# ConvNeXt-V2 block, one core: normalised rows on three of four partitions, their writes on ScalarE's queue, part of the bias add on VectorE, every third block stored whole

## The chip, the core and the metric

The kernel runs on one NeuronCore of a Trainium2 chip. The time is device microseconds (us) of one execution. The engines are PE (TensorE, matmul), ACT (ScalarE), DVE (VectorE), POOL (GpSimd) and SP (SyncE, which here only issues transfers); each takes its instructions in program order. Transfers issued by SP, ACT or POOL run on the same 16 DMA engines.

## The reference

The input is an image of 512 x 512 pixels with 96 channels, in bf16.

```python
out = depthwise 3x3 convolution of x           # 9 shifted products, per channel
h = layernorm(out) over the 96 channels        # no gain, no bias
h = gelu(h @ w1)                               # 96 -> 384
gx = sqrt(sum over all pixels of h*h + 1e-6)   # per hidden channel: needs the whole image
nx = gx / (mean of gx over channels + 1e-6)
h = gamma * (h * nx) + beta + h
return x + h @ w2                              # 384 -> 96
```

The sum over all pixels splits the work in two: nothing of the last product can start before every pixel's `h` has been made once.

## The kernel before

A block is four image rows (2048 pixels); there are 128 blocks. The kernel has two stretches.

**First stretch.** Slots `s` (loop at L826) each do several things for different blocks, one slot apart: load x of block s+4; transpose it on DVE (`turn_x`); convolve block s on PE and evacuate it with ACT (`y_bf`); square it on POOL (`ysq`) and sum over channels on PE; for each batch of four blocks make 1/sqrt(variance) in a dozen small POOL steps (`stage_rstd`, `stage_newton`), write it to DRAM and read it back spread over partitions (`stage_rows`, `stage_bcast`, tile `rbc`); multiply on POOL (`stage_norm`, tile `yn`); write `yn` to DRAM in four transfers, one for each image row (`stage_write`); one slot later read it back with the 96 channels on partitions 0 to 95 (`stage_read`, tile `ynT`); two slots after the read multiply it with w1 on PE and apply gelu on ACT (tile `g`). In a steady slot ACT does one `y_bf` and eight gelu activations: two-bank ones for units 0, 4 and 8, one-bank ones for units 2, 3, 6, 7, 10 and 11, with `y_bf` between units 7 and 8. Sums of squares come from DVE (`bst`, bn_stats) for the first two to four quarters of a block and from PE (`gram`) for the rest; `cm_quads` says how many.

What is kept for the second stretch differs by block. A whole block (`is_whole`: number modulo 10 is 0, 3 or 7, and below 114; 35 blocks) has its `g` written to DRAM in three parts (`store_next`, tile `g_dram`, one part a slot). Five blocks are held in SBUF. For the other 88 only `yn` is in DRAM, and `g` is made again.

All SP transfers stand in one queue in this order in a slot: load x, read `ynT`, write `yn` (four), `rbc`, rows, store. A transfer waits, in its queue, for what it depends on, and everything behind it waits too.

**Second stretch** (loop at L1008, `ORDER` mixes the kinds of blocks evenly). For each block: `load_rest` fetches `gl` (a whole block, POOL's queue) or `ynT` (SP's queue; 128 rows of 2048 values, that is the 96 of this block and the first 32 of the next, whose rows of w1 are zero); `load_xr` fetches x again (POOL's queue); POOL adds the bias to x (`stage_xb`, tile `xb`, f32); PE multiplies `ynT` with w1 again and ACT applies gelu (tile `gr`, four activations of 128x1536 a block); PE multiplies with the scaled w2 in four sub-blocks of 12 matmuls each, into one of two PSUM banks by turns; DVE adds `xb` and writes `o_sb`; SP writes `o_sb` out. There are four `o_sb`, five `xr` and three `xb` buffers.

In the built program each SP or ACT transfer also waits for an earlier one that used the same of eight semaphores; that is mostly the transfer eight before it in the common order of both queues.

Of the kernel before, what the change touches and what calls it, by code (L numbers as in the profile page):

```python
# [8 lines left out]
ALU = mybir.AluOpType  # L9
# [9 lines left out]
NHELD = 5  # L19
WHOLE = (0, 3, 7)  # L20
NTAIL = 14
# [35 lines left out]
def kernel(  # L57
# [39 lines left out]
    def is_whole(q):  # L97
        return q < TAIL0 and q % 10 in WHOLE

    def cm_quads(q):  # L100
        if is_whole(q) or is_held(q):
            return NQ
        if q > HELD[0]:
            return 1
        return 2 if q >= NBLK - 16 or (q - 1) % 10 in WHOLE else 3

# [15 lines left out]
    def yn_src(q):  # L122
        return yn_dram[q].rearrange("c (r w) -> c r w", r=GR)

    def yn_rows(q):
        return yn_dram[q:q + 2].rearrange("q c (r w) -> (q c) r w", r=GR)[0:128]

# [10 lines left out]
    rowsel = consts.tile([128, GR], bf16, name="rowsel")  # L138
    w1_raw = consts.tile([C, E], bf16, name="w1_raw")
    w1p = consts.tile([128, E], bf16, name="w1p")  # L140
# [43 lines left out]
    with ExitStack() as p1:  # L184
# [68 lines left out]

        cen = consts.tile([C, 128], bf16, name="cen")
        xtpool = pc.enter_context(tc.tile_pool(name="xt", side="right", bufs=1))
# [27 lines left out]
        def load_rest(n, sq, pq):  # L283
            q = ORDER[n]
            v = grp.setdefault(q, {})
            if is_held(q):
                v["g"] = gs[q]
            elif is_whole(q):
                v["g"] = late.gl.tile([128, NQ, NCH, QW], bf16, name="gl")
                pq.dma_start(out=v["g"][:].rearrange("p t j w -> p (t j w)"), in_=g_dram[whole.index(q)])  # L290
            else:
                ynt = yn_ring[SLOTS[nth_made[q] % NYT]]
                if q not in KEPT:
                    sq.dma_start(out=ynt[:], in_=yn_rows(q))
                v["ynt"] = ynt
# [24 lines left out]
        def stage_xb(q, pq, bias):  # L320
            if q is None:
                return
            xb = late.xb.tile([128, PXP, C], f32, name="xb")
            pq.tensor_tensor(out=xb[:], in0=grp[q]["xr"][:],  # L324
                                    in1=bias[:, None, :].to_broadcast([128, PXP, C]), op=ALU.add)
            grp[q]["xb"] = xb

        def stage_mm2(n, q):
# [3 lines left out]
            for sub in range(NSUB):  # L332
                O = out_bank()
                for gl_ in range(GPS):
                    gg = sub * GPS + gl_
                    for j in range(NCH):
                        t, c = gg // GQ, gg % GQ * 128
                        pe.matmul(O[:, gl_, :], lhsT=g[:, t, j, c:c + 128], rhs=W2s[:, j, :],
                                   start=(j == 0), stop=(j == NCH - 1))
                dve.tensor_tensor(out=o_sb[:, sub * GPS:(sub + 1) * GPS, :], in0=O,  # L340
                                   in1=xb[:, sub * GPS:(sub + 1) * GPS, :], op=ALU.add)
                if n == NBLK - 1:
# [44 lines left out]
        pool.memset(cen[:], 1.0)  # L387
        pool.memset(w1p[C:128, :], 0.0)
        dve.memset(SG, 0.0)
# [24 lines left out]
        for i in range(NI):  # L414
            act.dma_start(out=w1_raw[i:C:NI, :], in_=w1[chans(i), :])
        act.dma_start(out=w2_sb[:], in_=w2.rearrange("(j p) c -> p j c", p=128))
# [4 lines left out]
        def setup_ynt():  # L421
            for t in yn_ring:
                pool.memset(t[C:128, :, :].rearrange("p r w -> p (r w)").bitcast(f32), 0.0)

        def setup_mlp():
# [6 lines left out]
            dve.scalar_tensor_tensor(out=w1p[:C, :], in0=w1m[:C], scalar=-1.0 / C, in1=w1_raw[:],  # L432
                                     op0=ALU.mult, op1=ALU.add)
# [392 lines left out]
        for s in range(last_slot + 1):  # L826
            get = lambda kind: at.get((s, kind), [])
            if s + 4 < NBLK:
                load_x(s + 4)
            for b in get("read"):  # L830
                stage_read(b)
            for b in get("write"):
                stage_write(b)
            for k in get("bcast"):
                stage_bcast(k)
            for k in get("rows"):
                stage_rows(k)
            store_next()
            for k in get("newton"):
                stage_newton(k, pool)  # L840
# [4 lines left out]
            for k in get("rstd"):  # L845
                stage_rstd(k, pool)
            mlp = get("mlp")

# [36 lines left out]
            else:  # L885
# [4 lines left out]
                conv(0)  # L890
                unit(0, 2)
                unit(2, 1)
                squares(0)
# [158 lines left out]
```

## Time and profile before

| | |
|---|---|
| three timed runs | 1486.81, 1480.27, 1486.15 us; median 1486.15 |
| profiled execution, first to last instruction | 1480.8 us (the page gives no other time of it) |
| ACT busy | 1414.4 us (96%) |
| PE busy | 1391.3 us (94%) |
| POOL busy | 1300.3 us (88%) |
| DVE busy | 1182.0 us (80%) |
| granted PE clock | 0.994 |
| DMA | 433.08 MB, mean 292 GB/s |
| first stretch, steady part | about 120 to 880 us |
| second stretch | from 975 us, where the first `o_sb` is written |

The page's shares are over both stretches, which have different limits; the table by windows shows them apart. "Busy" of PE counts pipelined matmuls whose ends are modelled. A wait is put down to the semaphore that came last. Nearly all instructions carry L35, the line of the helper that records them, so they are told apart by tile.

### The profile page before, as it was taken

Reading aid. Unit: us, or ns where it says so; the run is one execution under the profiler, and the core shown is the slowest. Engines: PE = TensorE matmul, PEld = TensorE weight load, DVE = VectorE, ACT = ScalarE, POOL = GpSimd, SP = SyncE. Lnnn points to the kernel's source line nnn. Section 1 sums busy time; section 2 is a strip of 40 time slices with the busy share of each in tenths; the row PEclk is TensorE's granted clock in tenths of the full one; section 3 lists DMA queues with packets and bytes.
Section 4 is the critical chain, followed back from the end, with each engine's and each line's share of the span. In section 5 each row is a group of like instructions: output and inputs, shape, how many; then the busy total and the mean of one; then the engine's idle time right before and its main releaser. Section 6 shows DMA issues by size and latency. Waiting matters only on the chain.

```text
span 1480.8 us, 54225 instructions
## 1 busy us (share of the span) xinstructions
PE 1391.3 (94%) x23125; PEld 810.4 (55%) x23125; DVE 1182.0 (80%) x2135; ACT 1414.4 (96%) x1595; POOL 1300.3 (88%) x922
## 2 busy tenths in 40 slices
PE   8888999999999999999999997789999999999998
PEld 3434444444444444444444445467777777776776
DVE  7849989999999999999999987965555555555555
ACT  7888989999999999999999999999999999999997
POOL 3459889998998999998999987569999999999997
PEclk9999999999999999999999999999999999999999
DMA  5568788788888888888888866669999999999997
GB/s 180 179 205 255 241 253 280 228 271 260 260 248 264 258 264 255 276 253 254 263 258 266 263 216 195 195 225 409 366 359 402 417 416 413 419 410 417 411 412 282
DMA packets 167768, 433.08 MB, mean 292 GB/s; under 512 B 31558, under 2 KB 81318, under 8 KB 163046
## 3 DMA queue, kind: packets, MB, share of 16 engines
q1 hardware_dynamic: 151284, 326.04, 66.3%
q0 software_dynamic: 14880, 103.43, 17.6%
q8 instruction: 181, 2.97, 0.8%
q14 instruction: 61, 0.50, 0.1%
q10 hardware_dynamic: 1362, 0.15, 0.1%
HBM read 273.30 MB, written 156.22 MB: 290 GB/s over the span
## 4 chain that ended last, share of the span: by engine, by line
PE 30%; ACT 24%; DMA 19%; POOL 13%; DVE 6%; issue 4%; SPq 4%; POOLq 0%; ACTq 0%; DVEq 0%
PE PS L35 30%; ACT g L35 16%; DMA out_dram<-o_sb 9%; POOL yn L35 6%; ACT y_bf L35 5%; POOL ysq L35 5%; SPq L35 4%; DMA yn_dram<-yn 3%; DVE bst L35 3%; DMA xin<-in_x_dram 2%; DMA rbc<-r_dram 2%; DMA ynT<-yn_dram 1%; DMA g_dram<-g 1%; DVE o_sb L35 1%; ACT xT L35 1%
## 5 line engine op out<-in xcount | busy, mean ns | idle before, releaser
L35 ACT ACTIVATE g<-PS 128x512 bf16<-128x512 f32 (+2 forms) x1062 | 727.7, 864 | 16.5 <-PE PS L35 15.6
L35 DVE BATCH_NORM_STATS2 bst<-g 128x6 f32<-128x512 bf16 x1110 | 671.3, 672 | 35.4 <-ACT g L35 34.5
L35 PE MATMUL PS<-ynT,w1p 128*128 128x512 bf16 x2181 | 609.6, 381 | 23.6 <-ACT g L35 5.4
L35 ACT ACTIVATE gr<-PS 128x1536 bf16<-128x1536 f32 x360 | 498.5, 1459 | 18.8 <-PE PS L35 13.8
L35 POOL TENSOR_TENSOR yn<-y_bf,rbc 128x1536 bf16<-128x1536 bf16 x126 | 391.3, 3108 | 77.3 <-ACT rbc L35 21.9
L35 DVE TENSOR_TENSOR o_sb<-PS,xb 128x384 bf16<-128x384 f32 x512 | 277.3, 556 | 227.0 <-PE PS L35 190.1
L324 POOL TENSOR_TENSOR xb<-xr,B2c 128x1536 f32<-128x1536 bf16 x118 | 368.1, 3133 | 4.3 <-DVE o_sb L35 2.0
L35 PE MATMUL PS<-xT,Wq 64*32 64x511 bf16 (+1 forms) x9198 | 340.5, 389 | 26.2 <-ACT y_bf L35 8.1
L35 POOL TENSOR_TENSOR ysq<-y_bf 128x1536 bf16<-128x1536 bf16 x114 | 313.6, 2752 | 12.8 <-ACT y_bf L35 12.8
L35 PEld LDWEIGHTS <-w1p 128*128 128x128 bf16 x2181 | 171.6, 98 | 222.0 <-issue 133.4
L35 PEld LDWEIGHTS <-gr 128*128 128x128 bf16 x4296 | 212.1, 98 | 68.9 <-issue 12.0
L35 PE MATMUL PS<-W2s,gr 128*128 128x96 bf16 x4224 | 223.5, 206 | 8.2 <-DVE o_sb L35 8.0
L35 PEld LDWEIGHTS <-Wq 64*32 64x32 bf16 x9216 | 111.9, 90 | 193.3 <-issue 145.9
L35 ACT ACTIVATE y_bf<-PS 128x1536 bf16<-128x1536 f32 (+2 forms) x135 | 199.4, 1482 | 17.4 <-PE PS L35 13.3
L35 DVE STREAM_TRANSPOSE xT<-xin 128x576 f32<-128x576 f32 (+1 forms) x256 | 181.4, 748 | 8.1 <-DMA xin<-in_x_dram 8.1
L35 PEld LDWEIGHTS <-g 128*128 128x128 bf16 x1704 | 104.9, 98 | 86.3 <-issue 54.3
L35 PE MATMUL PS<-w1p,ynT 128*128 128x256 bf16 (+2 forms) x822 | 125.8, 273 | 8.0 <-ACT xT L35 3.2
L35 PE MATMUL PS<-g 128*128 128x128 bf16 x1464 | 122.6, 220 | 2.9 <-DVE PS L35 2.6
L35 PEld LDWEIGHTS <-gl 128*128 128x128 bf16 x1680 | 82.8, 98 | 26.8 <-issue 5.0
L35 PE MATMUL PS<-W2s,gl 128*128 128x96 bf16 x1680 | 89.5, 206 | 3.4 <-DVE o_sb L35 3.2
L35 PEld LDWEIGHTS <-ynT 128*128 128x128 bf16 x822 | 64.1, 97 | 31.5 <-issue 13.7
L279 POOL DMA_DIRECT2D xr<-in_x_dram x115 | 63.7, 555 | 14.2 <-POOL xb L324 14.2
(105 smaller groups left out, 576.5 us busy)
## 6 DMA issues: line engine op xcount, KB each, us to landing
xin<-in_x_dram SPq DMA_DIRECT2D x126, 432.0 KB
g_dram<-g SPq DMA_DIRECT2D x105, 512.0 KB
gl<-g_dram POOLq DMA_DIRECT2D x35, 1536.0 KB, 11.3
yn_dram<-yn SPq DMA_DIRECT2D x512, 96.0 KB
ynT<-yn_dram SPq DMA_DIRECT2D x128, 384.0 KB
out_dram<-o_sb SPq DMA_DIRECT2D x127, 384.0 KB
xr<-in_x_dram POOLq DMA_DIRECT2D x123, 384.0 KB, 6.9
ynT<-yn_dram SPq DMA_DIRECT2D x85, 512.0 KB
```

The source lines that it names most:

```text
L35: r = f(*a, **k)
L279: pq.dma_start(out=xr[:], in_=x[0, r0:r0 + GR].rearrange("r w c -> (r w) c").rearrange("(p g) c -> p g c", g=PXP))
L324: pq.tensor_tensor(out=xb[:], in0=grp[q]["xr"][:], in1=bias[:, None, :].to_broadcast([128, PXP, C]), op=ALU.add)
```

## The change

Four things are changed.

1. `ynT` holds channel 3c+i on partition 4c+i, so three of every four partitions are in use over the whole range 0 to 127; w1 is laid out the same way, and the fourth partitions are zero. A read of a block (`read_yn`) is now three transfers of 32 rows, in both stretches, and in the second stretch no rows of the next block are read.
2. In slots of the first stretch that have gelu units of a block below 114, the four `yn` writes are issued by ACT, between its activations: after unit 0, after unit 4, after `y_bf`, after unit 8. SP's order becomes load x, `rbc`, rows, store, read. Other slots keep SP, with reads first.
3. In the second stretch POOL adds the bias to three of four sub-blocks only (12 of 16 pixels of a partition). For the fourth DVE adds the bias into PSUM and then x, two instructions for one. `xr` has six buffers in place of five, since it is read until the block's end.
4. Whole blocks are those whose number is divisible by 3: 38 in place of 35, so 85 blocks are made again and not 88. `cm_quads` follows.

```diff
-WHOLE = (0, 3, 7)
+WHOLE = 3
     def is_whole(q):
-        return q < TAIL0 and q % 10 in WHOLE
+        return q < TAIL0 and q % WHOLE == 0
...
-        return 2 if q >= NBLK - 16 or (q - 1) % 10 in WHOLE else 3
+        return 2 if q >= NBLK - 16 or (q - 1) % WHOLE == 0 else 3
...
     def yn_src(q):
-        return yn_dram[q].rearrange("c (r w) -> c r w", r=GR)
-
-    def yn_rows(q):
-        return yn_dram[q:q + 2].rearrange("q c (r w) -> (q c) r w", r=GR)[0:128]
+        return yn_dram[q].rearrange("(c i) (r w) -> i c r w", i=NI, r=GR)
+
+    def read_yn(eng, t, q):
+        for i in range(NI):
+            eng.dma_start(out=t[i:128:4], in_=yn_src(q)[i])
...
                 if q not in KEPT:
-                    sq.dma_start(out=ynt[:], in_=yn_rows(q))
+                    read_yn(sq, ynt, q)
...
-            xb = late.xb.tile([128, PXP, C], f32, name="xb")
-            pq.tensor_tensor(out=xb[:], in0=grp[q]["xr"][:],
-                                    in1=bias[:, None, :].to_broadcast([128, PXP, C]), op=ALU.add)
+            n = PXP - GPS
+            xb = late.xb.tile([128, n, C], f32, name="xb")
+            pq.tensor_tensor(out=xb[:], in0=grp[q]["xr"][:, :n, :],
+                                    in1=bias[:, None, :].to_broadcast([128, n, C]), op=ALU.add)
...
+                add = xb
+                if sub == NSUB - 1:
+                    dve.tensor_tensor(out=O, in0=O, in1=B2c[:, None, :].to_broadcast([128, GPS, C]), op=ALU.add)
+                    add = grp[q]["xr"]
                 dve.tensor_tensor(out=o_sb[:, sub * GPS:(sub + 1) * GPS, :], in0=O,
-                                   in1=xb[:, sub * GPS:(sub + 1) * GPS, :], op=ALU.add)
+                                   in1=add[:, sub * GPS:(sub + 1) * GPS, :], op=ALU.add)
...
-        pool.memset(w1p[C:128, :], 0.0)
+        pool.memset(w1_raw[:], 0.0)
...
-            act.dma_start(out=w1_raw[i:C:NI, :], in_=w1[chans(i), :])
+            act.dma_start(out=w1_raw[i:128:4, :], in_=w1[chans(i), :])
...
-        def stage_write(b):
+        def write_parts(b, eng):
             yn = yns.pop(b)
-            for r in range(GR):
-                sp.dma_start(out=yn_dst(b, r), in_=yn[32 * r:32 * r + 32, :, :])
+            return [lambda r=r: eng.dma_start(out=yn_dst(b, r), in_=yn[32 * r:32 * r + 32, :, :]) for r in range(GR)]
...
-            sp.dma_start(out=t[:C], in_=yn_src(b))
+            read_yn(sp, t, b)
...
-            for b in get("read"):
-                stage_read(b)
-            for b in get("write"):
-                stage_write(b)
+            mlp = get("mlp")
+            steady = bool(mlp) and mlp[0] < TAIL0
+            wparts = [f for b in get("write") for f in write_parts(b, act if steady else sp)]
+            if not steady:
+                for b in get("read"):
+                    stage_read(b)
+                while wparts:
+                    wparts.pop(0)()
             for k in get("bcast"):
                 stage_bcast(k)
             for k in get("rows"):
                 stage_rows(k)
             store_next()
+            if steady:
+                for b in get("read"):
+                    stage_read(b)
...
                 unit(0, 2)
+                write_next()
                 unit(2, 1)
...
                 unit(4, 2)
+                write_next()
                 squares(1)
...
                     evac()
+                write_next()
                 gram_next(1 if taps else 2)
                 unit(8, 2)
+                write_next(len(wparts))
                 unit(10, 1)
...
-                late.xr = p2.enter_context(tc.tile_pool(name="xr", side="right", bufs=5))
+                late.xr = p2.enter_context(tc.tile_pool(name="xr", side="right", bufs=6))
```

More of the change, by code (lines that the diff above doesn't have):

```diff
@@ L138 @@
     rowsel = consts.tile([128, GR], bf16, name="rowsel")
-    w1_raw = consts.tile([C, E], bf16, name="w1_raw")
+    w1_raw = consts.tile([128, E], bf16, name="w1_raw")
     w1p = consts.tile([128, E], bf16, name="w1p")
@@ L252 @@
             dve.tensor_copy(out=eye32[32 * q:32 * q + 32, :], in_=ident_f[32 * q:32 * q + 32, 32 * q:32 * q + 32])
-        cen = consts.tile([C, 128], bf16, name="cen")
+        cen = consts.tile([128, 128], bf16, name="cen")
         xtpool = pc.enter_context(tc.tile_pool(name="xt", side="right", bufs=1))
@@ L422, in setup_ynt @@
             for t in yn_ring:
-                pool.memset(t[C:128, :, :].rearrange("p r w -> p (r w)").bitcast(f32), 0.0)
+                pool.memset(t[:].rearrange("p r w -> p (r w)").bitcast(f32), 0.0)
         def setup_mlp():
@@ L431, in setup_mlp @@
                           start=(j == 0), stop=(j == NCH - 1))
-            dve.scalar_tensor_tensor(out=w1p[:C, :], in0=w1m[:C], scalar=-1.0 / C, in1=w1_raw[:],
+            dve.scalar_tensor_tensor(out=w1p[:], in0=w1m, scalar=-1.0 / C, in1=w1_raw[:],
                                      op0=ALU.mult, op1=ALU.add)
@@ L838, with write_next @@
             store_next()
+            if steady:
+                for b in get("read"):
+                    stage_read(b)
+            def write_next(n=1):
+                for f in wparts[:n]:
+                    f()
+                del wparts[:n]
             for k in get("newton"):
@@ L846 @@
                 stage_rstd(k, pool)
-            mlp = get("mlp")
             def spread_out():
```

## The prediction

> **What bounds the kernel now.** I read the page first for the two stretches, then the busy time by windows for the engine that is full in each, then the waits, then SP's own waits, and last the timeline at the places that the change touches. Busy time by windows (PE, PEld, DVE, ACT, POOL, clock, DMA share, GB/s):
>
> ```profile
> core 0: us, PE busy (x) PEld busy (x) DVE busy (x) ACT busy (x) POOL busy (x), PEclk, DMA share, GB/s
> 320.00:480.00 160.00, 154.30 (x2805) 76.20 (x2790) 159.25 (x275) 160.00 (x228) 147.85 (x106) 1.00 0.83 258
> 480.00:640.00 160.00, 153.19 (x2772) 74.70 (x2772) 159.00 (x274) 159.05 (x227) 152.00 (x118) 1.00 0.83 260
> ```
> ```profile
> 1000.00:1440.00 440.00, 429.06 (x6255) 317.52 (x6252) 240.80 (x445) 423.19 (x307) 423.37 (x255) 1.00 1.01 405
> ```
>
> In the first stretch ACT is never idle (160.00 of 160), DVE hardly, and DMA has room (0.83). In the second, PE, ACT and POOL are each at 96 to 98%, the DMA engines are full, and only DVE has room (55%). Who waits there, from the list of waits (total, times, longest):
>
> ```profile
> DVE o_sb L35 <- DMA out_dram<-o_sb: 35.4, 24, 2.7
> ...
> ACT g L35 <- PE PS L35: 15.6, 15, 3.4
> ...
> PE PS L35 <- DVE o_sb L35: 11.3, 15, 1.6
> ```
>
> DVE waits for an output buffer whose write has not landed, PE then waits for DVE's bank: late transfers reach PE. The prices, from the page's groups and issues:
>
> ```profile
> L35 ACT ACTIVATE gr<-PS 128x1536 bf16<-128x1536 f32 x360 | 498.5, 1459 | 18.8 <-PE PS L35 13.8
> ...
> L35 DVE TENSOR_TENSOR o_sb<-PS,xb 128x384 bf16<-128x384 f32 x512 | 277.3, 556 | 227.0 <-PE PS L35 190.1
> L324 POOL TENSOR_TENSOR xb<-xr,B2c 128x1536 f32<-128x1536 bf16 x118 | 368.1, 3133 | 4.3 <-DVE o_sb L35 2.0
> ```
> ```profile
> gl<-g_dram POOLq DMA_DIRECT2D x35, 1536.0 KB, 11.3
> ...
> ynT<-yn_dram SPq DMA_DIRECT2D x85, 512.0 KB
> ```
>
> **The second stretch.** DMA: 85 reads of 512 KB (44.6 MB) become 82 reads of 384 KB (32.2 MB); three more whole blocks add 4.7 MB. That is 7.6 MB less; at the window's 405 GB/s, 18.8 us. ACT: three blocks fewer are made again, 12 activations at 498.5/360 = 1.385 us, 16.6 us less. PE: 36 matmuls of 512 columns fewer; three in a row span 0.81 us in the timeline and one record is 0.38, so they are 0.215 apart: 7.7 us less. PE idles 440 - 429.06 = 10.9 us in the window, so if every idle stretch went too PE could give 18.6 us, the same as DMA. POOL: 125 adds of 3.13 us lose a quarter, 98 us; POOL stops being one of the full engines, so its own 16.6 us of idle and its pace no longer matter.
>
> DVE: one more add of 0.557 us a block, 71 us over 128 blocks. In the window (440 us, 112 blocks at 3.9 us) that is 62 us, from 55% to 69%: room enough, but not free of effect. The bank of the last sub-block is held for two adds, 1.11 us, where it was held for 0.56. PE wants that bank again after one sub-block of 12 matmuls (24 in a row span 1.18 us, so 0.51) and, in two blocks of three, one group of three remaking matmuls (0.65): 1.16 us. So the second add is just covered, and where it is not PE loses up to 0.1 us, with 0.6 where no group lies between. Bounds 0 and 128 x 0.1 = 13 us; I take 3, since the average fits. The three reads for one cost SP two more issues of 0.33 us a block, in a queue that mostly waits for `o_sb`; reads are issued five blocks (20 us) ahead, which hides them unless SP is held by an earlier transfer. `xr` is released a block later and has a sixth buffer for it: 0.
>
> Bounds of the stretch: the limits of DMA and PE (18.8) less nothing, and PE's 7.7 alone less 13, that is 5 us worse. I take 15 us gained: the common limit less 3 for the bank, and a little of the late writes left.
>
> [...]
>
> **The first stretch.** What moves is 440 `yn` writes out of SP's queue into ACT's, the full engine. Four prices.
>
> (a) The issue. A write's issue takes 0.598 us (median of 379 between 160 and 840 us, longest 2.7): 263 us of ACT's queue in all. Whether ACT computes meanwhile is seen at the start, where ACT issues loads behind activations:
>
> ```profile
> 5.42 0.44 ACT L35 ACTIVATE Wq<-g 32x288 bf16<-32x288 bf16 x1 [1.46 <-DVE g L35]
> 5.59 0.59 ACTq L35 DMA_DIRECT2D w_raw<-in_w_dram  x1
> 5.77 0.88 ACT L35 ACTIVATE Wq<-g 32x288 bf16<-32x288 bf16 x2
> ```
>
> In program order the loads follow all six activations, yet the first issue runs while the first of them does: the queue issues while the engine works off what it has in hand. Each new write stands behind an activation of 1.1 us (two banks) or 1.56 us (`y_bf`), longer than 0.6. Bounds 0 and 263; I take 0, by this row, the same engine and the same operation. If that cover is gone, each write costs 0.6 us.
>
> (b) The wait for `yn`. The first write of a slot waits for POOL, and behind it stand unit 2 and all later activations. POOL after a batch's small steps, and ACT in the same slot:
>
> ```profile
> 516.40 3.11 POOL L35 TENSOR_TENSOR yn<-y_bf,rbc 128x1536 bf16<-128x1536 bf16 x1
> ```
> ```profile
> 515.52 5.94 ACT L35 ACTIVATE g<-PS 128x1024 bf16<-128x1024 f32 x9
> ```
>
> `yn` is ready at 519.51. The nine activations are units 8, 10, 11 and then 0, 2, 3, 4, 6, 7 of the next slot; unit 0 starts at 517.5 and unit 2 at 518.4. With the write between them unit 2 would start at 519.51 + 0.6: 1.7 us lost. That is one slot in four, 27 batches: upper bound 46 us. But a lost 1.7 us stays gained for POOL, whose work for four slots takes 27.6 us (from one batch's small steps at 511.88 to the next at 539.49) where ACT's takes 28.2 (`y_bf` at 507.12, 514.19, 521.25). One delay serves all later batches. I take 3.
>
> (c) The wait for an earlier transfer on the same semaphore. A slot had about 8.5 transfers and will have 10.5, so the one eight before is about 7.05 x 8/10.5 = 5.4 us old. The chain of waits shows pieces of 5.89 us for an x load and 7.03 for a `ynT` read, so some writes will come up to 1.6 us too early, and ACT has 0.5 to 1.6 us in hand. Bounds 0 and one such wait of 1.1 us in each of 110 slots, 121; I take 4, since a 128 KB read and a write that no longer stands behind three others should land sooner than those pieces.
>
> (d) What SP gets back:
>
> ```profile
> SPq L35 <- DMA yn_dram<-yn: 133.5, 149, 3.8
> ...
> SPq L35 <- POOL yn L35: 64.3, 39, 4.2
> ```
>
> SP stands 64 us for POOL's `yn`, with `rbc`, rows and stores behind it, and POOL waits for `rbc` 21.8 us in turn. With the writes gone `rbc` goes out at once and POOL runs earlier, which helps (b). For the end only ACT's idle time counts: 680 - 671.04 = 9.0 us between 160 and 840 us. Bounds 0 and 9; I take 4.
>
> [...]
>
> Edits taken at nothing: 4.7 MB more stores (DMA share 0.83 covers them), three bn_stats fewer, memsets over 128 partitions (POOL is done with them by 12.2 us and next waits for ACT until 34.2), the w1 load behind a memset that ends before 2.8 us.
>
> Net of the first stretch: +3 + 4 - 4 = 3 us worse.
>
> **Sum.** -15 + 3 = -12 us. Against the profiled execution, 1480.8 - 12 = 1468.8. Its span lies 5.35 us under the median of the runs shown, near the fastest of them, so for the median I say 1486.15 - 12 = 1474 us.
>
> **Rivals.** A difference of 0.5% is 7.4 us, about what three runs of this kernel can tell from none.
>
> Slower: ACT's queue becomes the bound of the first stretch. One mechanism, (c): reads wait for the last write, the write of the next slot waits for a read, the x load stands behind both. For it: ACT has no idle time, two more transfers a slot, landings of 6 to 7 us. Against: 5.4 us and what ACT has in hand cover most. At 0.3 us a slot it is 33 us: 1486 - 15 + 33 = 1504. It decides from 22.4 us on, 0.2 us a slot.
>
> Faster by more: (b) and (c) cost nothing, ACT's 9 us of idle go, and the second stretch gains the whole 18.8: 1486 - 28 = 1458. For it: POOL and SP are relieved in both stretches.
>
> No change: the second stretch gives PE's 7.7 alone, since ACT and PE at 97% hold each other, and the first costs 8 by (b) and (c): 1486.
>
> **How the numbers follow.** Forecast 0.44 (own range 1466 to 1478), faster by more 0.15, no change 0.17, slower 0.24. So faster 0.59, same 0.17, slower 0.24. The range 1456 to 1500 reaches the middle of the faster case and most of the slower one; about 0.2 stays outside.
>
> **What would show it.** Right: between 1000 us and the end DMA share still near 1 but `o_sb` waiting less than 35 us for output, POOL near 78%, 348 `gr` activations; in the first stretch `y_bf` still every 7.05 us and ACT idle under 10 us. Wrong: `y_bf` further apart than 7.25 us with ACT's idle time ended by a transfer or by POOL's `yn` (the slower case); more than 13 us of PE waiting for `o_sb` (the bank). The prediction fails most easily if the earlier-transfer wait recurs in every slot.

## The result and the profile after

The changed kernel takes 1626.22 us (median, 1621.01 to 1630.46) against 1483.32 us (1480.26 to 1486.81) for the kernel before, measured beside it: a ratio of 1.0955, 95% interval 1.0927 to 1.0982. It is slower by 143 us, where 12 us less was forecast, and far outside the range of 1456 to 1500. The profiled execution has a span of 1628.4 us (before: 1480.8).

Both stretches lost. I count the second stretch from the first `o_sb` add to the last: it begins at 1099.4 us (before 975.5, so the first stretch is 123.9 us longer) and lasts 525.7 us (before 501.9, 23.8 longer).

The busy time by windows of the changed kernel: two windows of the first stretch, two of the second.

```profile
core 0: us, PE busy (x) PEld busy (x) DVE busy (x) ACT busy (x) POOL busy (x), PEclk, DMA share, GB/s
320.00:480.00 160.00, 139.66 (x2434) 67.76 (x2432) 140.56 (x239) 141.93 (x198) 131.92 (x100) 0.97 0.79 235
480.00:640.00 160.00, 139.61 (x2381) 66.51 (x2388) 137.43 (x232) 140.03 (x195) 126.56 (x99) 0.94 0.78 231
...
1240.00:1360.00 120.00, 117.19 (x1688) 85.51 (x1687) 82.71 (x152) 112.85 (x81) 93.46 (x71) 1.00 1.01 396
1360.00:1440.00 80.00, 76.60 (x1111) 56.07 (x1108) 53.33 (x99) 73.47 (x54) 54.31 (x42) 1.00 1.00 373
```

In the first stretch no engine is full any more: ACT, which had 160.00 of 160, has 141.93, and the DMA share fell with it. Every engine has room and the work is slower, so the time is in waits between them. `y_bf` comes every 8.21 us on the mean between 320 and 800 us, against 7.10, and ACT idles 58.7 of these 480 us, against 3.9. In the second stretch the DMA share is still 1.0, yet the rate is 373 to 396 GB/s where it was 414 in both windows. The kernel before, in its second stretch:

```profile
1120.00:1240.00 120.00, 116.87 (x1703) 86.46 (x1702) 64.89 (x121) 115.11 (x84) 116.71 (x70) 1.00 1.02 413
1240.00:1360.00 120.00, 116.66 (x1690) 85.83 (x1689) 65.42 (x122) 114.71 (x84) 116.09 (x72) 1.00 1.02 414
1360.00:1440.00 80.00, 77.08 (x1126) 57.12 (x1125) 43.38 (x81) 76.13 (x56) 76.63 (x47) 1.00 1.02 414
```

The waits of the changed kernel over the whole run (total, times, longest):

```profile
POOL yn L35 <- DMA yn_dram<-yn: 76.6, 32, 4.5
POOL xb L326 <- DMA xr<-in_x_dram: 51.8, 15, 4.9
...
ACT g L35 <- PE PS L35: 44.4, 67, 2.1
ACT g L35 <- DMA ynT<-yn_dram: 39.2, 29, 2.8
...
DVE o_sb L35 <- POOL xb L326: 26.8, 24, 2.9
...
PE PS L35 <- DVE o_sb L35: 18.9, 16, 2.2
```

and SP's own:

```profile
SPq L35 <- DMA yn_dram<-yn: 356.4, 132, 7.7
```

ACT, whose activations need no transfer, waits for `ynT` reads: these are its writes, standing in its queue. DVE's wait for output buffers is nearly gone (35.4 to 2.8 us), and another has come: POOL for `xr`, and DVE for POOL's `xb`. SP's wait for POOL's `yn` is gone (64.3 to 2.5), its wait for the landing of `yn` writes is up from 133.5 to 356.4. One slot in the timeline, ACT and then SP:

```profile
606.59 0.56 ACTq L35 DMA_DIRECT2D yn_dram<-yn  x1
607.19 1.09 ACT L35 ACTIVATE g<-PS 128x512 bf16<-128x512 f32 x2
608.16 1.46 ACT L35 ACTIVATE y_bf<-PS 128x1536 bf16<-128x1536 f32 x1
611.57 0.56 ACTq L35 DMA_DIRECT2D yn_dram<-yn  x1
612.17 1.02 ACT L35 ACTIVATE g<-PS 128x1024 bf16<-128x1024 f32 x1 [2.56 <-DMA ynT<-yn_dram]
```
```profile
602.59 0.38 SPq L35 DMA_DIRECT2D g_dram<-g  x1
609.21 1.73 SPq L35 DMA_DIRECT2D ynT<-yn_dram  x3
```

SP stood from 602.97 to 609.21 for the last write of the block that it was to read; ACT had issued that write at 602.56, and it landed at 609.06. SP's reads went out at 609.21, the first of them landed at 611.54, and ACT's next write, which shares a semaphore with it, could be issued only at 611.57. ACT had been free since 609.62.

### The profile page after: what moved, and what is told of

Read it like the earlier page. It is cut to its first block, busy times and chain, and to the rows that moved or that the text cites. A ratio compares the mean times of both kernels' runs of the same rounds, so it can differ in the third digit from the quotient of the medians.

```text
span 1628.4 us, 55038 instructions
## 1 busy us (share of the span) xinstructions
PE 1431.7 (88%) x23104; PEld 822.3 (50%) x23104; DVE 1265.6 (78%) x2260; ACT 1423.6 (87%) x1583; POOL 1205.0 (74%) x925
## 4 chain that ended last, share of the span: by engine, by line
PE 24%; DMA 19%; DVE 6%; ACT 5%; POOL 2%; SPq 2%; issue 2%; ACTq 1%; POOLq 0%; DVEq 0%
PE PS L35 24%; DMA xr<-in_x_dram 6%; ACT g L35 4%; DMA ynT<-yn_dram 4%; DMA yn_dram<-yn 4%; DVE o_sb L35 3%; DVE PS L35 2%; SPq L35 2%; DMA xin<-in_x_dram 2%; DMA out_dram<-o_sb 1%; DMA g_dram<-g 1%; ACTq L35 1%; POOL xb L326 1%; ACT y_bf L35 1%; POOL yn L35 1%
## 5 line engine op out<-in xcount | busy, mean ns | idle before, releaser
L35 DVE BATCH_NORM_STATS2 bst<-g 128x6 f32<-128x512 bf16 x1107 | 679.0, 673 | 148.1 <-ACT g L35 147.2
L35 PE MATMUL PS<-ynT,w1p 128*128 128x512 bf16 x2142 | 621.2, 390 | 113.9 <-ACT g L35 83.4
L35 ACT ACTIVATE gr<-PS 128x1536 bf16<-128x1536 f32 x348 | 488.6, 1449 | 51.0 <-PE PS L35 45.9
L35 PE MATMUL PS<-xT,Wq 64*32 64x511 bf16 (+1 forms) x9198 | 348.8, 397 | 30.9 <-ACT y_bf L35 16.0
L326 POOL TENSOR_TENSOR xb<-xr,B2c 128x1152 f32<-128x1152 bf16 x118 | 280.5, 2392 | 86.7 <-DMA xr<-in_x_dram 51.8
L35 DVE TENSOR_TENSOR o_sb<-PS,xb 128x384 bf16<-128x384 f32 x384 | 209.1, 556 | 124.4 <-PE PS L35 83.9
L35 ACT ACTIVATE y_bf<-PS 128x1536 bf16<-128x1536 f32 (+2 forms) x135 | 191.3, 1422 | 17.7 <-PE PS L35 13.4
L35 PE MATMUL PS<-W2s,gl 128*128 128x96 bf16 x1824 | 100.6, 208 | 23.4 <-DVE o_sb L35 18.4
L35 PEld LDWEIGHTS <-gl 128*128 128x128 bf16 x1824 | 91.5, 99 | 52.9 <-issue 29.5
L35 DVE TENSOR_TENSOR PS<-PS,B2c 128x384 f32<-128x384 f32 x128 | 72.5, 566 | 50.9 <-PE PS L35 50.9
```

The source lines that it names most:

```text
L35: r = f(*a, **k)
L326: pq.tensor_tensor(out=xb[:], in0=grp[q]["xr"][:, :n, :], in1=bias[:, None, :].to_broadcast([128, n, C]), op=ALU.add)
```

## The experiments

Times are set against runs of the kernel before on the same chip. The table has the stretches (us), each from one profiled execution. How far these can be trusted: eight kernels of this document, the one before among them, have the same second stretch, and it lasted 501.2 to 505.2 us. For late_xr and three_plain the profiled execution was the fastest of its kernel, 10 and 7 us below the median.

| kernel | second stretch begins | lasts | ratio of times (95%) |
|---|---|---|---|
| before | 975.5 | 501.9 | 1 |
| changed | 1099.4 | 525.7 | 1.0955 (1.0927 to 1.0982) |
| writes_only | 1041.8 | 502.0 | 1.0418 (1.0368 to 1.0468) |
| layout_only | 1043.8 | 497.3 | 1.0411 (1.0367 to 1.0454) |
| adds_only | 979.1 | 523.4 | 1.0177 (1.0135 to 1.0219) |
| whole_only | 975.0 | 507.6 | 1.0018 (0.9988 to 1.0047) |
| after_writes_sp | 1046.3 | 522.3 | 1.0564 (1.0520 to 1.0607) |
| after_one_layout | 1039.4 | 530.7 | 1.0622 (1.0568 to 1.0676) |
| three_plain | 1020.5 | 501.5 | 1.0345 (1.0289 to 1.0401) |
| writes_read_later | 1104.7 | 502.7 | 1.0881 (1.0837 to 1.0925) |
| writes_early | 1202.4 | 505.2 | 1.1551 (1.1501 to 1.1601) |
| second_add | 976.1 | 511.8 | 1.0063 (1.0035 to 1.0091) |
| late_xr | 974.5 | 509.5 | 1.0094 (1.0065 to 1.0122) |
| reads_96 | 972.0 | 525.6 | 1.0135 (1.0100 to 1.0169) |
| layout_second | 985.4 | 497.2 | 0.9994 (0.9972 to 1.0017) |
| layout_second_b | 975.8 | 497.1 | 0.9974 (0.9950 to 0.9998) |

### The four parts, one at a time

**Only the writes on ScalarE's queue** (writes_only: the kernel before, plus this; an excerpt):

```diff
+            wparts = [f for b in get("write") for f in write_parts(b, act if steady else sp)]
...
                 unit(0, 2)
+                write_next()
...
```


> The kernel before with one part of the change: in the steady slots the four yn writes of a block are issued from ScalarE's queue at the new places, and the read of a slot goes out behind the broadcast, the rows and the stores. The ynT reads stay single transfers of 96 rows, so a slot has about 8.5 transfers and not 10.5. In the changed kernel the second stretch began at 1099.4 us and before at 975.5: 123.9 us were lost in about 110 steady slots, 1.1 us a slot. Theory 1 (ScalarE waits at a write for an earlier transfer, read or write, whatever the number of reads): this part alone costs at least 60 us, y_bf periods of 7.6 us or more, total 1545 or more. Theory 2 (the two added reads are what fills SP's queue and the semaphores; the move of the writes alone is harmless): within 15 us of before, y_bf periods of 7.1 us. Theory 3 (the two need each other): 10 to 50 us. The second stretch should stay at 502 us under all three.

1547.49 us: the first stretch loses 66.3 us, the second nothing. Theory 1 holds in size: this part is enough alone. (It also puts the read behind `rbc`, rows and store in SP's order, as the changed kernel does; that was not tried by itself.) Its waits:

```profile
ACT g L35 <- DMA ynT<-yn_dram: 26.0, 13, 3.2
...
ACT g L35 <- DMA yn_dram<-yn: 8.7, 3, 3.6
```
```profile
SPq L35 <- DMA yn_dram<-yn: 454.6, 163, 9.5
```

I followed every write through the semaphore that it shares. Between 320 and 800 us 15 of 246 writes left ACT idle for more than 0.1 us before they were issued (I call these held up), 17.0 us together, and each was issued 0.02 to 0.08 us after the landing of the transfer that had used its semaphore before: ten were `ynT` reads, issued by SP after 4 to 7 us of standing, within 0.15 us of the landing of a `yn` write that ACT had issued 5 to 7 us earlier. None came with POOL's `yn`. The issue behind a late write is not covered: 9.0 us for the 15, that is 0.60 each. The other 231 left ACT idle for 7.4 us, 0.03 each.

**Only the layout** (layout_only: three reads for one, in both stretches; writes on SP; an excerpt):

```diff
+    def read_yn(eng, t, q):
+        for i in range(NI):
+            eng.dma_start(out=t[i:128:4], in_=yn_src(q)[i])
...
-            sp.dma_start(out=t[:C], in_=yn_src(b))
+            read_yn(sp, t, b)
```


> The kernel before with one part of the change: yn on three of four partitions, so that each ynT is read by three transfers of 32 rows, from SP's queue as before; the writes stay on SP. A slot of the first stretch then has about 10.5 transfers. Theory 1 (the loss is in ScalarE's queue): first stretch as before, second stretch begins at 975 to 985 us. Theory 2 (the reads fill SP's queue and the semaphores): SP, which stood 133 us for its own yn writes, stands much longer and the first stretch loses 60 us or more. Theory 3 (the two need each other): 0 to 30 us lost. For the second stretch, which took 525.7 us in the changed kernel against 501.9: if the three spread reads slow the transfers down (262 us of them more in packets of gl, 547 ns against 482), it is longer by 15 to 30 us here already; if the other parts do it, it gains some 10 us from 11 MB less read.

(The "262 us" in it is a slip; nothing rests on it.) 1546.98 us: 68.3 us lost in the first stretch, 4.6 gained in the second. Theory 2 is right here in the loss, without any write on ACT, but not in its sign: SP did not stand longer for its `yn` writes. SP issues transfers for 406.9 of the 480 us between 320 and 800 us, against 336.4: 6.4 us a slot of 7.56 and not 5.0 of 7.10. A read's issue takes 0.60 us on the mean, three times, where the single one took 0.45. SP's wait for `yn` writes fell from 133.5 to 67.4 us. The end of that chain in the waits (all of the run), first of layout_only, then of the kernel before:

```profile
ACT g L35 <- PE PS L35: 63.6, 50, 5.3
...
POOL yn L35 <- DMA rbc<-r_dram: 49.8, 15, 10.4
...
PE PS L35 <- POOL ysq L35: 45.5, 25, 5.8
```
```profile
POOL yn L35 <- DMA rbc<-r_dram: 21.8, 9, 7.2
...
PE PS L35 <- POOL ysq L35: 10.2, 5, 4.0
```

`rbc` comes late, POOL's `yn` and the `ysq` behind it are late, PE waits for POOL, and ACT waits for PE (15.6 us before).

**Only VectorE's adds and the sixth `xr` buffer** (adds_only; the excerpt leaves out POOL's shorter add and the buffer).

```diff
+                if sub == NSUB - 1:
+                    dve.tensor_tensor(out=O, in0=O, in1=B2c[:, None, :].to_broadcast([128, GPS, C]), op=ALU.add)
+                    add = grp[q]["xr"]
```


> The kernel before with one part of the change: for the last sub-block of each block VectorE adds the bias and then x itself, GpSimd prepares three quarters of xb, and xr has a sixth buffer. The first stretch is not touched: second stretch from 975 us. If the later release of xr and the bank held for two adds are what makes the second stretch longer in the changed kernel, it grows here by 10 to 25 us, with GpSimd waiting for xr (51.8 us in the changed kernel). If they are hidden, as the forecast took, the time is within 5 us of before, GpSimd near 78% busy.

1510.81 us, and the loss is in the second stretch: +21.5 us. This part is what the second stretch of the changed kernel lost, though POOL has 87.68 of 120 us busy where it had 116.71.

**Only every third block stored whole** (whole_only; an excerpt).

```diff
-WHOLE = (0, 3, 7)
+WHOLE = 3
```


> The kernel before with one part of the change: every third block is stored whole, 38 in place of 35. 4.7 MB more are written in the first stretch and read in the second, three 512 KB reads fewer, 12 activations of 1.385 us and 36 matmuls of 512 columns fewer in the second stretch. By the forecast's rows: DMA +4.7 - 1.6 = 3.1 MB, 8 us more at 405 GB/s, against 8 to 17 us less of TensorE and ScalarE: between 8 us slower and 8 us faster, by whether the DMA or the engines bound. The even spacing in place of 0, 3, 7 of ten should change nothing.

1486.16 us, no change that can be told: the interval of the ratio allows 2 us less to 7 us more. The profiled execution has 5.7 us more in the second stretch, although 12 activations and 36 wide matmuls are fewer.

By stretch the four nearly add up: in the first 66.3 + 68.3 + 3.6 - 0.5 = 137.7 (together 123.9), in the second 0.1 - 4.6 + 21.5 + 5.7 = 22.7 (together 23.8).

### Two parts undone

The changed kernel with the writes back on SP (after_writes_sp), and the changed kernel with the old layout and single reads (after_one_layout), both as excerpts.

```diff
-            wparts = [f for b in get("write") for f in write_parts(b, act if steady else sp)]
...
+            for b in get("write"):
+                stage_write(b)
```


> The changed kernel with one part undone: the writes are back on SP's queue, in the order of before. One part alone cost 66.3 us (writes) and 68.3 us (layout) in the first stretch, and both together 123.9; in the second stretch writes 0, layout -4.6, VectorE's adds +21.5, every third block whole +5.7, and all four together +23.8. Theory 1 (the parts add up): the second stretch begins at 1040 to 1050 us (68 late), lasts 520 to 528 us, total 1562 to 1580. Theory 2 (one cause, SP's full queue, of which each part is a different view): it begins well below that, under 1025 us, or takes back less than 40 us of the changed kernel's loss, over 1060.

```diff
-                    read_yn(sq, ynt, q)
+                    sq.dma_start(out=ynt[:], in_=yn_rows(q))
```


> The changed kernel with the other part undone: yn on the 96 partitions of before, one transfer for each read, while the writes stay on ScalarE's queue. If the parts add up, the second stretch begins at 1035 to 1050 us, as with the writes moved alone, and lasts some 529 us (+21.5 and +5.7 without the layout's -4.6): total 1568 to 1585. If it is the three issues of a read that make ScalarE's waits what they are, the second stretch begins below 1025 us.

1570.47 and 1575.54 us. Undoing the writes gives back 53.1 us of the first stretch, undoing the layout 60.0: two losses, not two views of one. But the layout's loss has another form beside the writes: SP then issues for 219.3 of 480 us only and is not full. Between 320 and 800 us POOL waits 55.3 us for buffers that a `yn` write still holds (18.9 with the old layout) and ACT's held-up writes are 27 with 22.5 us (23 with 18.2). That this comes of the thirds' later landing is likely, not shown.

### Number of reads or layout

Three_plain is the kernel before with each read of the first stretch split in three, on the old partitions.

```diff
+            for i in range(NI):
+                sp.dma_start(out=t[32 * i:32 * i + 32], in_=yn_src(b)[32 * i:32 * i + 32])
```


> The kernel before with each ynT read of the first stretch cut in three transfers of 32 rows; the rows stay on partitions 0 to 95, so the layout is that of before, and the reads of the second stretch are left single. The kernel with only the new layout lost 68 us in the first stretch; SP's issues took 407 of 480 us there between 320 and 800 us (6.5 us a slot) against 336 (4.9 us a slot). Theory 1 (the number of issues fills SP's queue): the same 55 to 70 us are lost here, the second stretch begins at 1030 to 1046 us. Theory 2 (the spread partitions themselves make the transfers slow): it begins at 975 to 990 us.

1535.06 us; the second stretch begins 45.0 us late, between the two. The number of issues makes about two thirds of the layout's 68.3 us. The rest goes with the spread rows, whose issues are longer: 0.60 us against 0.45 for a third of plain rows, so that a slot's reads add 1.36 us of issuing to SP's queue in layout_only and 0.89 in three_plain. The two losses stand in the same ratio as these two numbers, which speaks for the time of issuing, without proving it.

### Why ScalarE's writes wait

Both kernels are writes_only with one more change: the reads one slot later (writes_read_later), or the writes earlier (writes_early).

```diff
-                put(s + 2, "read", b)
+                put(s + (2 if ramp else 3), "read", b)
```


> The kernel with only the writes moved to ScalarE's queue, and on top of that each ynT read is put one slot later (it still has a slot before the block's matmuls). In the kernel with only the writes moved, SP stood 454.6 us for yn writes that ScalarE had just issued, and ScalarE stood 26 us for ynT reads at its own writes; its second stretch began at 1041.8 us, 66 us late. Theory 1 (a closed loop: ScalarE's last write of a slot lands, only then SP issues the read, and the next slot's write stands for that read on the shared semaphore): the read finds its write landed, the loop opens, SP's wait for yn falls below 150 us and at least 45 of the 66 us come back; second stretch from 975 to 995 us. Rival A (ScalarE pays for the issue, 0.60 us for each of four writes a slot, or for GpSimd's yn, whatever the reads do): the second stretch still begins at 1030 us or later. Rival B (eight semaphores are shared whatever the order): between the two, 1000 to 1030.

```diff
                 unit(0, 2)
-                write_next()
+                write_next(2)
...
```


> As with only the writes moved to ScalarE's queue (second stretch from 1041.8 us), but two of the four writes stand at the first place and two at the second, none later. Between 320 and 800 us 15 of that kernel's writes were held up, each until 0.02 to 0.08 us after the landing of the transfer that used its semaphore before, ten of them a ynT read that SP had issued late, because it stood 4 to 7 us for the last, fresh write. Theory 1 (fresh writes hold SP, SP's late read holds the next write): with the last write some 4 us earlier SP finds it landed, its wait for yn falls from 455 us to 250 or less, and 30 to 60 of the 66 us come back: second stretch from 980 to 1010 us. Rival A (issuing four times 0.6 us on ScalarE's queue is itself the cost): two writes in a row are less covered than one, and it begins at 1040 us or later. Rival B (some other transfer takes the read's place on the semaphore, as when the reads were put later): 1020 us or later, with ScalarE waiting for an x load, rows or a store.

My theory 1 fell here. Each should have spared SP the standing behind a fresh write; 1614.91 and 1714.33 us were measured, worse than with the writes moved alone, although SP's wait for `yn` writes went from 454.6 to 194.4 us with later reads (with earlier writes only to 399.6). The waits, first of the later reads, then of the earlier writes:

```profile
ACT g L35 <- DMA xin<-in_x_dram: 58.9, 25, 4.1
```
```profile
SPq L35 <- DMA yn_dram<-yn: 194.4, 57, 9.5
SPq L35 <- DVE rt L35: 161.3, 24, 10.3
```
```profile
ACT g L35 <- DMA yn_dram<-yn: 87.1, 17, 6.5
...
ACT g L35 <- DMA rbc<-r_dram: 39.2, 9, 6.0
```

With later reads another transfer took the read's place: the held-up writes (31, 31.4 us between 320 and 800 us) wait for rows (5.2 us), before which SP had stood 7 to 12 us, and for the x loads behind them (25.8). With earlier writes there are 28, and 52.2 us when the idle time of two writes in a row is counted once; the list of waits puts most of it down to the `yn` writes themselves, but followed through the semaphores 25.6 us are still for `ynT` reads and 20.5 for `rbc`. Rival A has a part in it: ACT was idle for another 37.3 us of these 480 while it issued (14.7 in writes_only), where the second of two writes has no activation to cover it. Again each of these was issued within 0.08 us of the landing of the transfer before it on the same semaphore. So what holds ACT is not one loop through the read: a write in ACT's queue stands for whatever transfer is about eight before it, and that one stands in SP's queue behind anything SP waits for.

**Fewer transfers: one write for four.** This was to lift the transfer eight before out of reach. First at the first place (writes_one), then at the last (writes_one_late), then on SP with the new layout (layout_writes_one), then on SP with the old (sp_writes_one). (The first expectation speaks of 24 held-up writes in writes_only; the trace shows 15.)

```diff
-            return [lambda r=r: eng.dma_start(out=yn_dst(b, r), in_=yn[32 * r:32 * r + 32, :, :]) for r in range(GR)]
+            return [lambda: eng.dma_start(out=yn_dram[b].rearrange("(c i) (r w) -> r c i w", i=NI, r=GR), in_=yn[:])]
```


> As the kernel with only the writes moved to ScalarE's queue (second stretch from 1041.8 us, 66 us late, 24 of its 246 writes between 320 and 800 us held up), but the block's yn goes out as one transfer in place of four, at the first of the four places. A slot then has about 5.5 transfers, and the one eight before is over a slot old. Theory 1 (a write on ScalarE's queue stands for the transfer eight before it, which may itself stand in SP's queue behind something late): ScalarE's waits for transfers go below 10 us in all and the second stretch begins at 975 to 990 us. Rival A (ScalarE pays for the issue itself: 384 pieces then take four times 0.6 us in one): 1030 us or later. Rival C (the write waits for GpSimd's yn, and all the waiting now falls on this first place): 990 to 1025, with ScalarE's idle time ended by yn.

> The same single write at the last of the four places, behind the activation of banks 8 and 9, so that SP's read at the start of the next slot comes as soon after the write as with the writes moved alone. It tells the two halves of theory 1 apart. If the number of transfers is what matters (eight semaphores), the second stretch begins at 975 to 995 us although SP stands for the fresh write; if it is SP's standing behind a fresh write that makes everything late, 1010 us or later, and SP's wait for yn stays above 300 us.

> As the kernel with only the new layout (three reads for one; second stretch from 1043.8 us, 68 us late, SP issuing for 407 of 480 us), but the block's yn goes out from SP's queue as one transfer in place of four. If SP's queue was full because of the number of issues, about 2 us of issuing a slot go, SP issues for some 290 of 480 us and the second stretch begins at 975 to 985 us; the second stretch stays at 497 us, so the total is some 1473 to 1482, below the kernel before by up to 8. If one issue of four times the pieces takes four times as long, or the three reads for other reasons hold the first stretch, it begins at 1020 us or later.

> The kernel before with the block's yn written by one transfer in place of four, on SP's queue as before: the control of the run above. SP was not full before (336 of 480 us), so the forecast is no change, 975 us to the second stretch and a total within 8 us of before; a gain of up to 9 us (ScalarE's idle time in the first stretch) if GpSimd's wait for the broadcast rows, which stand behind the writes, was worth anything.

1700.35, 1798.04, 1940.77 and 1783.06 us (ratios 1.150, 1.216, 1.312 and 1.205, each within 0.007): all far slower, the control too, so these tell nothing of the number of transfers. The single write is a slow transfer. On SP it lands 8.8 us (median) after its issue, where each of the four took 3.5 to 4.4, and x loads and stores land later beside it: after 8.3 us in place of 6.0, and 7.8 in place of 3.9. Its semaphore is counted up in 5 steps in the trace, where that of each of the four, of a read or of an x load takes 16. The DMA engines meanwhile have more room than before: their share between 320 and 640 us is 0.61 to 0.64 in sp_writes_one and was 0.83. Which of the engines a transfer ran on no trace here shows, so why the single write is slow was not shown.

What did come out: with the same single write, the late place costs 98 us more than the early one, so the place of a write does matter where its landing is slow.

### The second stretch

Part three was split in two: the second add alone (second_add), and the late use of `xr` without it (late_xr; the excerpt leaves out POOL's shorter add and the sixth buffer).

```diff
+                if sub == NSUB - 1:
+                    dve.tensor_tensor(out=O, in0=O, in1=zero_c[:, None, :].to_broadcast([128, GPS, C]), op=ALU.add)
```


> The kernel before with one more add of VectorE on the bank of each block's last sub-block (zeros, so the sum stays); GpSimd prepares all of xb and xr keeps its five buffers as before. The kernel with part three alone had a second stretch of 523.4 us against 501.9. Theory 1 (VectorE's second pass: the bank held for two adds, or its work beside the transfers): 515 to 525 us here too. Theory 2 (what costs is that xr is released only after the last sub-block, so that its next load and with it all of GpSimd's queue starts later): 500 to 506 us.

```diff
+                add = xb
+                if sub == NSUB - 1:
+                    add = grp[q]["xr"]
```


> The other half of part three: GpSimd adds the bias to three quarters of x, VectorE takes the last quarter straight from xr, which is released after that, with six buffers; the extra bias add is left out, so the output lacks the bias in every fourth sub-block. Theory 1 (VectorE's second pass is the cost): a second stretch of 495 to 506 us. Theory 2 (the late release of xr is the cost): 515 to 525 us, with GpSimd waiting for xr some 70 us as in the whole part.

Neither theory alone: 1494.33 and 1498.92 us, +9.9 and +7.6 us in the stretch, of 21.5 for the whole part. (By the ratios of the times the three are 9, 14 and 26 us.) The second add costs by itself, with nothing else changed. In its trace 96 of the 128 blocks are followed by a product that starts 0.05 us after the doubled add has ended, 25.2 us later in all than the usual spacing of the matmuls, 0.26 us each; before, 25 products started late behind an add, by 15.3 us. PE waits for the bank, in gaps too short for the list of waits. The late release shows as a chain in late_xr, POOL for `xr` and DVE for POOL (0.9 us before):

```profile
POOL xb L325 <- DMA xr<-in_x_dram: 85.5, 27, 5.5
...
DVE o_sb L35 <- POOL xb L325: 35.0, 19, 3.1
```

PE's listed wait for `o_sb`, first in second_add, then in late_xr:

```profile
PE PS L35 <- DVE o_sb L35: 1.6, 3, 0.7
```
```profile
PE PS L35 <- DVE o_sb L35: 19.0, 20, 2.0
```

**Bytes or layout** (reads_96).

```diff
-                    sq.dma_start(out=ynt[:], in_=yn_rows(q))
+                    sq.dma_start(out=ynt[:C], in_=yn_src(q))
```


> The kernel before with one size changed: in the second stretch each read takes the 96 rows that are needed (384 KB) and not 128 rows (512 KB), still as one transfer of partitions 0 to 95. It separates the bytes from the layout: 85 x 128 KB = 11.1 MB less. If the DMA engines' bytes set the second stretch, as the forecast's -18.8 us took it, 11.1 MB at 413 GB/s are 27 us, and with TensorE and ScalarE at 97% perhaps 10 to 18 of them are gained: second stretch 484 to 492 us against 501.9. If the rate falls as it did with the new layout (413 to 393-399 GB/s), it gains 5 us or less: 496 to 503.

1504.31 us: 11.1 MB fewer, and the stretch is 23.7 us longer. Neither bound that I gave has it. Windows of this kernel:

```profile
1120.00:1240.00 120.00, 112.93 (x1592) 82.59 (x1590) 61.43 (x114) 107.92 (x79) 111.54 (x70) 0.97 1.02 373
1240.00:1360.00 120.00, 111.78 (x1601) 82.33 (x1598) 60.99 (x113) 108.15 (x79) 108.07 (x65) 0.99 1.02 367
```

The DMA share is 1.02 as before, the rate 373 and 367 where it was 413 and 414, and a packet of 4096 bytes takes 195 ns on the mean between 1080 and 1440 us, before 163. The same 96 rows spread over three of four partitions, in three transfers (layout_only), took 28.3 us less than packed ones in one. So the new reads gain against packed rows; the kernel before, with its 128-row reads, had most of that already. Whether the partitions or the number of transfers make the difference, and what the lower granted clock of 0.97 to 0.99 adds, was not separated.

**The spread reads in the second stretch alone**, with a second copy of the weights (`w1s`), first made in slot 4 (layout_second), then in slot 40 (layout_second_b); an excerpt:

```diff
+                    for i in range(NI):
+                        sq.dma_start(out=ynt[i:128:4], in_=yn_dram[q].rearrange("(c i) (r w) -> i c r w", i=NI, r=GR)[i])
```


> The new layout in the second stretch alone: the first stretch reads 96 partitions in one transfer as before, and the reads of the second stretch put yn on three of four partitions in three transfers, against a second copy of the weights on the same rows. With the layout everywhere the first stretch lost 68 us and the second gained 4.6. If the two have nothing to do with each other: second stretch from 975 to 980 us, lasting 494 to 500, total 2 to 8 us below the kernel before. If the gain there came from the first stretch's end (blocks kept, a queue drained), 500 to 506 us and no gain.

> The new layout in the second stretch alone, once more: the first stretch of that kernel began its second stretch at 985.4 us and not 975.5, because the three small copies of the weights stood in SP's queue in the fourth slot (that slot took 15.2 us instead of 9.2) . Here they are issued in slot 40, when the weights have long been ready. If that was all, the second stretch begins at 974 to 978 us and lasts 495 to 499 us: total 3 to 8 us below the kernel before, a ratio of 0.994 to 0.998, the only version here that would be below it. If the gain of the spread reads is not real, 0.999 to 1.002.

1484.95 and 1480.11 us. In the profiled execution the copies in slot 4 cost the first stretch 9.9 us and hid the gain; in slot 40 they cost nothing. The last one is the only version below the kernel before, and only just: 0.9974, interval 0.9950 to 0.9998, about 4 us, near the 4.8 that its second stretch lasts less.

## Why the prediction was wrong

- **Second stretch, DMA's -18.8 us at 405 GB/s.** The step took a share near 1 for a limit in bytes. Shares of 1.00 to 1.02 stood beside 365 to 419 GB/s in these runs: with other rows or pace the same share moved less. The layout gave 4.6 to 4.8 us in three kernels; every third block gave nothing that can be told (5.7 us worse in one profile).
- **ACT -16.6, PE -7.7.** The count of `gr` activations went to 348 as said, but whole_only shows no gain from it.
- **The bank held for two adds, 3 (bounds 0 to 13).** Right mechanism, mis-sized: +9.9 us in second_add, where PE started 0.26 us late behind 96 doubled adds and not by 0.1 at most. The bound of 13 also left out the prediction's own case of 0.6 us where no group lies between, one block in three, some 26 us. The sign named, more than 13 us of PE waiting for `o_sb`, came (18.9 us, before 11.3) but does not tell of the bank: the list has 1.6 us in second_add and 19.0 in late_xr, which has no second add.
- **`xr`'s sixth buffer, 0.** Wrong: +7.6 us in late_xr by its profile, 14 by its times. I counted buffers, and not that the next load and all of POOL's queue now start after the block's last add. Before, `xr` was free after POOL's add, which is made two blocks ahead; so the release is nearly three blocks later, not one, for one more buffer. POOL's relief, some 88 us of `xb` adds, shows as a gain in no run.
- **Three reads for one, 0.** The largest miss: 68.3 us. The step priced two more issues in the second stretch only, and at 0.33 us, the single read's median; they took 0.60 us each. In the first stretch, where SP already issued for 5.0 us of each 7.1, the added issues were given no term.
- **First stretch, (a) the issue, 0.** Right while the write is on time: 0.03 us each. It costs 0.60 behind each late one.
- **(b) POOL's `yn`, 3.** No held-up write in writes_only ended with `yn`.
- **(c) the earlier transfer, 4 (bounds 0 and 121).** This is the step that failed in kind as well as size. The wait recurs, as the prediction's last sentence feared. It reckoned the age of the transfer eight before from its place in the order, 5.4 us; what counts is when SP issued it, and SP stood for 4 to 7 us first. Whole cost of the writes: 66.3 us, 0.6 us for each of 110 slots, of which 0.43 us is seen directly at ACT between 320 and 800 us (17.0 + 9.0 us over 61 slots); the rest was not traced to single waits. The slower rival had this mechanism at 0.3.
- **(d) SP relieved, -4.** Opposite: SP's time stood in waits for the fresh writes (133.5 to 454.6 us in writes_only). No gain was seen in the first stretch, 66.3 us longer there; the cost was in the waits that came to stand in the computing engine's queue (17.0 us at ACT between 320 and 800 us).

## What to carry to other kernels

Before a transfer is moved to a computing engine's queue, follow for each one the earlier transfer that shares its semaphore, to the queue where it is issued and to everything that queue waits for; the computing engine inherits those waits (17.0 us at ACT between 320 and 800 us in writes_only), and here moving the reads or the writes in time only exchanged one for another. Price an added issue in every stretch, at the duration of its own shape (here 0.60 us a read, where 0.33 was reckoned), against what its queue already issues in a period. A DMA share of 1 is not a rate (365 to 419 GB/s stood beside 1.00 to 1.02 here): look at the rate with the new rows before turning fewer bytes into time.

## What the hardware showed that was not expected

- One transfer of 384 KB, a block's four image rows in one, lands after 8.8 us, and x loads and stores land later beside it (8.3 and 7.8 us, before 6.0 and 3.9); four of 96 KB, same bytes and same 1 KB pieces, land after 3.5 to 4.4 us each.
- Reads of 96 packed partitions made the second stretch 23.7 us longer than reads of 128 partitions with a third more bytes.
- The granted clock fell with the waits: 0.994 before, 0.969 after (0.94 to 0.97 in its first stretch, 1.00 in its second), 0.888 in the slowest kernel, layout_writes_one. What part of the loss is the clock's was not separated.
